# Retention followed by mixture-of-depths: one 128-row matmul for the output in place of two 64-row ones

## The chip, the core and the metric

The kernel runs on one core of a Trainium2 chip. The metric is device time in microseconds (us) for one execution: the median of several runs.

## The reference

Eight batches, eight heads, 576 positions, head dimension 64. The first part is retention in its parallel form: scores `q k^T`, times a decay `gamma_h ** (i - j)` for `i >= j` and 0 elsewhere, times the values. The heads are then put side by side (512 columns), and in every batch the 128 rows with the highest gate score go through a two-layer network of width 1024.

```python
gamma = 1.0 - 2.0 ** (-5.0 - np.arange(H))
rel = pos[:, None] - pos[None, :]
Dmat = np.where(rel >= 0, gamma[:, None, None] ** rel[None, :, :], 0.0)
attn = np.matmul(scale * np.matmul(q, k.T) * Dmat, v)      # per batch and head
x = attn.transpose(0, 2, 1, 3).reshape(B, S, H * D)
...
scores = np.einsum('bsd,d->bs', x, w_gate)
out = x.copy()
for b in range(B):
    top_idx = np.argpartition(-scores[b], capacity)[:capacity]
    xe = x[b, top_idx]
    ye = np.maximum(xe @ w1, 0.0) @ w2
    out[b, top_idx] = xe + sigmoid(scores[b, top_idx])[:, None] * ye
```

## The kernel before

Retention is computed in chunks of 64 positions, nine to a batch (`NC`), 72 in all. A chunk `g` is chunk `c` of batch `b` (`batch(g)`). Within a chunk the kernel takes scores, masks them and multiplies them by the values; what earlier chunks give comes from a 64x64 state per head, the running sum of key times value. The decay is split: values are divided by `gamma ** t` at the chunk's position in its batch (`scaled`, tile `vs`), and the output is multiplied by `gamma ** t` again (`values`).

Two chunks make a step `s` (36 steps, chunks `2s` and `2s + 1`, called `e` = 0 and 1). The 128 partitions hold the positions of a chunk twice over: the lower 64 belong to four of the heads (`HH`) and the upper 64 to the other four (`halves`). A retention matmul is therefore 64 rows by 64 columns and 64 columns of moving data, and runs in one quarter of the TensorE array. Matmuls that stay in their half (`scores`, line 185, and `update`, line 175) use two quarters; those that cross over (`crosswise`, lines 196 and 206, which write the output `y_ps`) use the two others.

`block(s)` writes the order of TensorE's retention work for a step out by hand. It takes two matmul calls at a time from each of two lists. The first, `diagonal`, holds the update of the state with chunk `2s - 1` (8 calls), the scores of step `s` (16) and the update with chunk `2s` (8). The second, `crosswise(s - 1)`, holds masked scores times values for the step before (16 calls) and queries times state (16, fewer where a batch begins). All data is 32-bit float, and each call shows in the trace as two matmul instructions with two weight loads.

The state of all heads accumulates in one PSUM bank, `u_ps`, over a batch. After each update ScalarE copies it to SBUF (`copied`, line 215, tile `st`), and the next update may not write the bank before that copy has read it. The copy of chunk `2s - 1` is issued in the middle of `block(s)`, that of chunk `2s` at its end. VectorE then masks the scores (`masked`, line 242, tile `am`), scales the output (`values`, line 251), and takes the gate scores (line 260). GpSimd scales the values (line 161; in some steps, `by_act`, ScalarE does it with eight instructions, line 157) and issues the stores of the output (line 268). SyncE issues the loads: four transfers of 256 KB for each step (`load`: queries, keys turned, values, keys), eight steps ahead (`AHEAD`, the buffers of the pool `loads`), with a limit on the transfers in flight (`few`).

Between blocks TensorE works off the pieces of the two-layer network of an earlier batch (`up`, line 379, and `down`, line 387, handed out by `some`), and the ranking of a batch's gate scores: `total` (line 293), `spread` (line 308), `compare` (VectorE, line 321), `one_hot` and `rows` (line 342), then an indirect transfer that gathers the chosen rows (`gather`, line 353), `turn` (line 370) and `gates`. `first` and `second` are the hand-ordered steps 4 and 5 at the end of the first batch; `mid`, `early` and `late` are lists of what else is issued in a step. No scheduler reorders anything: each engine runs its instructions in the order in which the program issues them.

Of the kernel before, what the change touches and what calls it, by code (L numbers as in the profile page):

```python
# [35 lines left out]
def kernel(  # L36
# [28 lines left out]
    NK = (NC + 1) // 2  # L65
    W = HH * D
# [2 lines left out]
    col = layout(H, NC, cap)  # L69

    const = ctx.enter_context(tc.tile_pool(name="const", bufs=1))
    loads = ctx.enter_context(tc.tile_pool(name="loads", bufs=8))
    work = ctx.enter_context(tc.tile_pool(name="work", bufs=3))
    psum = ctx.enter_context(tc.tile_pool(name="psum", bufs=2, space=PSUM))

# [52 lines left out]
    slots = const.tile([P, cap], F32, name="slots")  # L128
    eye = const.tile([P, P], F32, name="eye")
    ones = const.tile([P, P], F32, name="ones")  # L130

    def constants():

# [11 lines left out]

    vs, am, sc_ps, y_ps, u_ps, st, xs, sc = {}, {}, {}, {}, {}, {}, {}, {}

    by_act = lambda s: ends[0] <= s < ends[0] + 3 or s - 3 in ends[1:-1]  # L150

    def scaled(s):
        c = batch(2 * s)[1]
        vs[s] = work.tile([P, DM], F32, name="vs")
        if by_act(s):
            for i in range(H):
                nc.scalar.activation(  # L157
                    out=vs[s][:, D * i : D * i + D], in_=raw[s][:, 2, D * i : D * i + D],
                    func=AF.Copy, scale=dec[:, 0, HH * c + i : HH * c + i + 1])
            return  # L160
        nc.gpsimd.tensor_tensor(  # L161
            out=blocks(vs[s]), in0=blocks(raw[s][:, 2, :]),
            in1=dec[:, 0, HH * c : HH * c + H].unsqueeze(2).to_broadcast([P, H, D]), op=OP.mult,
        )

    def update(g):

        (b, c), (s, e) = batch(g), divmod(g, 2)
        if c == NC - 1:
            return  # L170
        if c == 0:
            u_ps[b] = bank("u_ps", "u", 1)
        for h in range(HH):
            for half in halves:
                yield lambda h=h, half=half: nc.tensor.matmul(  # L175
                    u_ps[b][half, where(0, h)], raw[s][half, 3, where(e, h)],
                    vs[s][half, where(e, h)],
                    start=c == 0 and h == 0, stop=c == NC - 2, skip_group_check=True)

    def scores(s):  # L180
        sc_ps[s] = bank("sc_ps", "sc", 2)
        for e in range(2):
            for h in range(HH):
                for half in halves:
                    yield lambda e=e, h=h, half=half: nc.tensor.matmul(  # L185
                        sc_ps[s][half, where(e, h)], raw[s][half, 1, where(e, h)],
                        raw[s][half, 0, where(e, h)],
                        start=True, stop=True, skip_group_check=True)

    def crosswise(s, es=(0, 1)):  # L190
        if es[0] == 0:
            y_ps[s] = bank("y_ps", "y", 2)
        for e in es:
            for h in range(HH):
                for i, half in enumerate(halves):
                    yield lambda e=e, h=h, i=i, half=half: nc.tensor.matmul(  # L196
                        y_ps[s][halves[1 - i], where(e, h)], am[s][half, where(e, h)],
                        vs[s][half, where(e, h)],
                        start=e == 0 and h == 0, stop=False, skip_group_check=True)
        for e in es:  # L200
            g = 2 * s + e
            if batch(g)[1] == 0:
                continue
            for h in range(HH):
                for i, half in enumerate(halves):
                    yield lambda g=g, e=e, h=h, i=i, half=half: nc.tensor.matmul(  # L206
                        y_ps[s][halves[1 - i], where(e, h)], raw[s][half, 0, where(e, h)],
                        st[g - 1][half, where(0, h)], start=False, stop=True,
                        skip_group_check=True)

    def copied(g):
        b, c = batch(g)
        if c < NC - 1:
            st[g] = work.tile([P, W], F32, name="st")
            nc.scalar.copy(out=st[g], in_=u_ps[b][:, :W])  # L215
# [191 lines left out]

    AHEAD = 8  # L410

    def hidden(f):

# [21 lines left out]
    last = B - 1  # L435
    odd = (NC - 2) // 2

    def go(fs):
        for f in fs:
            f()  # L440

    def first():

        s = ends[0] - 1
        block(s)
        masked(s)
        go(crosswise(s, (0,)))
# [8 lines left out]
        go(crosswise(s, (1,)))  # L456
        for k in range(full):
            compare(0, k, 0, P * full)

# [12 lines left out]
    plan(mid, s, rows, 0)  # L472
    plan(mid, s, gather, 0)
    plan(mid, s, store, s - 2, (1,))
    then = {AHEAD: [(upper,)], AHEAD + 1: [(lower, 0)], AHEAD + 2: [(lower, FB // 2)]}
    for x in range(AHEAD, s + AHEAD):
        plan(mid, s, load, x)
        for f, *a in then.get(x, []):
            plan(mid, s, f, *a)
# [35 lines left out]

    bring(table, consts)
    constants()
    for s in range(AHEAD):
        load(s)
    hidden(0)  # L520
    scaled(0)
    for s in range(NS + 1):
        if s > ends[0] + 1 and s + AHEAD - 1 < NS:
            load(s + AHEAD - 1)
        run(before, s)
        if s + 1 < NS and not by_act(s + 1):
            scaled(s + 1)
        if s == ends[0] - 1:
            first()
        elif s == ends[0]:  # L530
            second()
        else:
            block(s)
            if s < NS:
                masked(s)
            run(mid, s)
            if s:
                values(s - 1)
# [4 lines left out]
        if by_act(s + 1) and s + 1 not in vs:  # L543
            scaled(s + 1)
        run(early, s)
        some(share.get(s, 0))
        run(late, s)
# [78 lines left out]
```

## Time and profile before

| | |
|---|---|
| median of 3 runs | 261.44 us (258.08 to 262.19) |
| time of the profiled execution | 259.97 us |
| its span, first to last instruction | 258.2 us |
| TensorE matmuls busy | 225.0 us, 87% (5143 instructions) |
| TensorE weight loads busy | 178.1 us, 69% (5143) |
| VectorE busy | 133.5 us, 52% |
| GpSimd busy | 97.6 us, 38% |
| ScalarE busy | 68.7 us, 27% |
| mean granted TensorE clock | 0.954 |

An engine's busy time is the time in which at least one of its instructions was running. Matmuls overlap: one 64x64 matmul lasts some 0.22 us, but several run at once, so a rate is read from the distance between starts and not from the duration. The clock is given as a share of full speed. In the profile "PE" is TensorE, "PEld" its weight loads, "DVE" VectorE, "ACT" ScalarE, "POOL" GpSimd and "SP" SyncE; "issue" as what ended a wait means that the profile shows no engine or transfer that was waited for.

### The profile page before, as it was taken

Reading aid. Unit: us, or ns where it says so; the run is one execution under the profiler, and the core shown is the slowest. Engines: PE = TensorE matmul, PEld = TensorE weight load, DVE = VectorE, ACT = ScalarE, POOL = GpSimd, SP = SyncE. Lnnn points to the kernel's source line nnn. Section 1 sums busy time; section 2 is a strip of 40 time slices with the busy share of each in tenths; the row PEclk is TensorE's granted clock in tenths of the full one; section 3 lists DMA queues with packets and bytes.
Section 4 is the critical chain, followed back from the end, with each engine's and each line's share of the span. In section 5 each row is a group of like instructions: output and inputs, shape, how many; then the busy total and the mean of one; then the engine's idle time right before and its main releaser. Section 6 shows DMA issues by size and latency. Waiting matters only on the chain.

```text
span 258.2 us, 11519 instructions
## 1 busy us (share of the span) xinstructions
PE 225.0 (87%) x5143; PEld 178.1 (69%) x5143; DVE 133.5 (52%) x354; ACT 68.7 (27%) x230; POOL 97.6 (38%) x132
## 2 busy tenths in 40 slices
PE   0757774896996999889999998999999999999991
PEld 0746654896656797569867976689769966874940
DVE  0344696052993439546835376559465494650201
ACT  2111373131240233313511334133412342221200
POOL 4336304333363541635083722551455505301101
PEclk9995998599797999999999999999999999999997
DMA  6887999999999898799789888986133214201101
GB/s 204 278 256 260 300 371 274 384 326 327 323 287 349 287 313 289 247 310 320 232 282 307 295 280 257 322 287 196 48 83 84 60 27 127 81 3 41 41 0 41
DMA packets 28240, 56.81 MB, mean 220 GB/s; under 512 B 4128, under 2 KB 4256, under 8 KB 28192
## 3 DMA queue, kind: packets, MB, share of 16 engines
q1 hardware_dynamic: 23328, 42.46, 50.3%
q0 software_dynamic: 4864, 13.64, 15.7%
q8 instruction: 40, 0.66, 1.0%
q14 instruction: 8, 0.07, 0.1%
HBM read 44.54 MB, written 11.53 MB: 217 GB/s over the span
## 4 chain that ended last, share of the span: by engine, by line
PE 69%; issue 11%; DMA 9%; ACT 3%; DVE 3%; POOLq 1%; POOL 1%; SPq 0%; ACTq 0%
PE h_ps L379 21%; PE ye_ps L387 16%; PE u_ps L175 10%; PE sc_ps L185 8%; DMA raw<-in_qkvk 7%; PE y_ps L206 5%; PE y_ps L196 3%; PE row_ps L308 3%; DMA xr<-out,idx 2%; PE xg_ps L370 2%; DVE scr L321 2%; ACT vs L157 1%; PE rs_ps L293 1%; PE idx_ps L342 1%; POOLq L564 1%
## 5 line engine op out<-in xcount | busy, mean ns | idle before, releaser
L242 DVE TENSOR_TENSOR am<-sc_ps,table 128x512 f32<-128x512 f32 x36 | 24.9, 691 | 81.4 <-PE sc_ps L185 67.4
L379 PEld LDWEIGHTS h_ps<-xg,w_sb 128*128 128x128 f32 x512 | 61.5, 197 | 5.7 <-issue 3.3
L379 PE MATMUL h_ps<-xg,w_sb 128*128 128x128 f32 x512 | 64.4, 284 | 0.9 <-ACT xg L371 0.7
L387 PE MATMUL ye_ps<-w_sb,hT 128*128 128x512 f32 x128 | 61.4, 611 | 0.0
L185 PE MATMUL sc_ps<-raw 64*64 64x64 f32 x1152 | 45.0, 227 | 10.1 <-DMA raw<-in_qkvk 7.2
L268 POOL DMA_DIRECT2D out<-xs x64 | 39.5, 620 | 35.6 <-DVE xs L251 35.5
L175 PE MATMUL u_ps<-vs,raw 64*64 64x64 f32 x1024 | 45.2, 228 | 6.6 <-ACT st L215 3.1
L185 PEld LDWEIGHTS sc_ps<-raw 64*64 64x64 f32 x1152 | 40.1, 141 | 13.5 <-issue 12.4
L196 PE MATMUL y_ps<-vs,am 64*64 64x64 f32 x1152 | 44.7, 225 | 5.1 <-issue 4.1
L175 PEld LDWEIGHTS u_ps<-vs,raw 64*64 64x64 f32 x1024 | 37.1, 140 | 14.7 <-issue 7.6
L215 ACT COPY st<-u_ps 128x256 f32<-128x256 f32 x64 | 23.8, 372 | 88.0 <-PE u_ps L175 59.7
L196 PEld LDWEIGHTS y_ps<-vs,am 64*64 64x64 f32 x1152 | 38.4, 137 | 5.9 <-issue 4.9
L161 POOL TENSOR_TENSOR vs<-raw,table 128x512 f32<-128x512 f32 x27 | 29.1, 1079 | 34.2 <-DMA raw<-in_qkvk 27.7
L206 PE MATMUL y_ps<-st,raw 64*64 64x64 f32 x1024 | 40.5, 227 | 1.3 <-issue 1.3
L321 DVE SCALAR_TENSOR_TENSOR scr<-row,rs,ahead 128x576 f32<-128x576 f32 (+5 forms) x47 | 34.8, 741 | 8.5 <-ACT row L313 5.8
L206 PEld LDWEIGHTS y_ps<-st,raw 64*64 64x64 f32 x1024 | 36.3, 142 | 0.8 <-issue 0.7
L387 PEld LDWEIGHTS ye_ps<-w_sb,hT 128*128 128x128 f32 x128 | 22.8, 195 | 19.5 <-issue 18.5
L260 DVE SCALAR_TENSOR_TENSOR scr<-xs,table 128x256 f32<-128x256 f32 x72 | 33.7, 468 | 2.5
L353 POOL DMA_INDIRECT xr<-out,idx x8 | 8.4, 1053 | 56.4 <-ACT idx L345 56.4
L381 ACT ACTIVATE hT<-h_ps 128x256 f32<-128x256 f32 x32 | 12.3, 383 | 52.8 <-PE h_ps L379 52.8
L251 DVE TENSOR_TENSOR xs<-y_ps,table 128x512 f32<-128x512 f32 (+1 forms) x37 | 24.7, 668 | 2.8 <-PE y_ps L206 2.5
L393 POOL DMA_INDIRECT out<-o,idx x8 | 9.5, 1189 | 25.6 <-DVE o L392 24.5
(34 smaller groups left out, 110.1 us busy)
## 6 DMA issues: line engine op xcount, KB each, us to landing
raw<-in_qkvk SPq DMA_DIRECT2D x144, 256.0 KB, 4.6
out<-xs POOLq DMA_DIRECT2D x64, 128.0 KB, 4.8
w_sb<-in_w SPq DMA_DIRECT2D x16, 256.0 KB, 5.6
out<-xs POOLq DMA_DIRECT2D x16, 64.0 KB, 4.4
wg<-in_w_gate SPq DMA_DIRECT2D x1, 256.0 KB
table<-in_consts SPq DMA_DIRECT2D x1, 234.5 KB
xr<-out,idx POOLq DMA_INDIRECT x8, 5.8
out<-o,idx POOLq DMA_INDIRECT x8, 4.0
```

The lines of the kernel that those rows point to most:

```text
L161: nc.gpsimd.tensor_tensor(out=blocks(vs[s]), in0=blocks(raw[s][:, 2, :]), in1=dec[:, 0, HH * c : HH * c + H].unsqueeze(2).to_broadcast([P, ...
L175: yield lambda h=h, half=half: nc.tensor.matmul(u_ps[b][half, where(0, h)], raw[s][half, 3, where(e, h)], vs[s][half, where(e, h)], start= ...
L185: yield lambda e=e, h=h, half=half: nc.tensor.matmul(sc_ps[s][half, where(e, h)], raw[s][half, 1, where(e, h)], raw[s][half, 0, where(e, h ...
L196: yield lambda e=e, h=h, i=i, half=half: nc.tensor.matmul(y_ps[s][halves[1 - i], where(e, h)], am[s][half, where(e, h)], vs[s][half, where ...
L206: yield lambda g=g, e=e, h=h, i=i, half=half: nc.tensor.matmul(y_ps[s][halves[1 - i], where(e, h)], raw[s][half, 0, where(e, h)], st[g - 1 ...
L242: nc.vector.tensor_tensor(out=blocks(am[s]), in0=blocks(sc_ps[s]), in1=causal.unsqueeze(1).to_broadcast([P, H, C]), op=OP.mult)
L251: nc.vector.tensor_tensor(out=blocks(xs[s])[:, i0:i1, :], in0=blocks(y_ps[s])[:, i0:i1, :], in1=dec[:, 1, HH * c + i0 : HH * c + i1].unsqu ...
L260: nc.vector.scalar_tensor_tensor(scr, xs[s][:, W * e : W * e + W], 1.0, wgh, op0=OP.mult, op1=OP.mult, accum_out=sc[b][:, c : c + 1])
L268: nc.gpsimd.dma_start(out=outs[b][C * c : C * c + 2 * C, W * i : W * i + W] .rearrange("(c p) d -> p c d", c=2), in_=xs[s][half, :].rearra ...
L321: nc.vector.scalar_tensor_tensor(scr[:n, : j1 - j0], row[b][:n, j0:j1], rs[b][:n, k : k + 1], ahead[:n, at + j0 : at + j1], op0=OP.subtrac ...
L379: nc.tensor.matmul(t[:, a, :], w1_sb[:, d, P * (f + a) : P * (f + a) + P], xg[b][:, d, :], start=d == 0, stop=d == KD - 1)
L387: nc.tensor.matmul(ye[b], hT[b][:, a, :], w2_sb[:, a, :], start=a == 0, stop=a == FB - 1)
```

## The change

Masked scores and queries are put one under the other in the 128 partitions, and so are values and state, so that one matmul with 128 rows gives what two with 64 rows gave before. For this a step's tile `raw` has six slots in place of four. For the lower half the slots 2 and 3 are loaded with queries and values, for the upper half the slots 4 and 5. The masked scores of one half are written by VectorE beside the queries of the other (`masked`, slots `QA`), and the copy of the state goes beside the values of the other half (`copied`, slots `VS`), which takes two ScalarE instructions of 64 partitions in place of one of 128. The weight `1 / gamma ** t` is no longer put on the values: for the scores it is in a table `decay` (mask times weight, made by VectorE in five instructions, `decays`), and for the state it is put on the keys, in place, by the engine that scaled the values before. The mask becomes two VectorE instructions. Scores now cross over between halves, so that scores and updates use the four quarters together, and the output's matmuls come after both. The loads are six steps ahead, with eight issued at the start; a load is still four transfers of 256 KB, now in the order keys turned, queries with values (one transfer for each half), keys.

```diff
-    loads = ctx.enter_context(tc.tile_pool(name="loads", bufs=8))
+    loads = ctx.enter_context(tc.tile_pool(name="loads", bufs=6))
...
+    KT, KN = 0, 1
+    QA, VS = {1: 2, 0: 4}, {0: 3, 1: 5}
...
     def load(s):
-        x = loads.tile([P, 4, DM], F32, name="raw")
-        for a in range(4):
-            bring(x[:, a, :], qkvk[s, :, a * DM : (a + 1) * DM], few=6 if ends[0] < s <= FEW else 4)
+        x = loads.tile([P, 6, DM], F32, name="raw")
+        few = 6 if ends[0] < s <= FEW else 4
+        src = qkvk[s].rearrange("p (a d) -> p a d", d=DM)
+        bring(x[:, KT, :], src[:, 1, :], few)
+        for p, half in enumerate(halves):
+            bring(x[half, QA[1 - p] : VS[p] + 1, :], src[half, 0:3:2, :], few)
+        bring(x[:, KN, :], src[:, 3, :], few)
...
+    def decays(c0, c1):
+        n = HH * (c1 - c0)
+        nc.vector.tensor_tensor(
+            out=decay[:, c0:c1, :].rearrange("p c (h d) -> p (c h) d", d=C),
+            in0=causal.unsqueeze(1).to_broadcast([P, n, C]),
+            in1=dec[:, 0, HH * c0 : HH * c1].unsqueeze(2).to_broadcast([P, n, C]), op=OP.mult)
...
     def scaled(s):
...
+        keys = raw[s][:, KN, :]
...
         nc.gpsimd.tensor_tensor(
-            out=blocks(vs[s]), in0=blocks(raw[s][:, 2, :]),
+            out=blocks(keys), in0=blocks(keys),
...
     def update(g):
...
-                    u_ps[b][half, where(0, h)], raw[s][half, 3, where(e, h)],
-                    vs[s][half, where(e, h)],
+                    u_ps[b][half, where(0, h)], raw[s][half, KN, where(e, h)],
+                    raw[s][half, VS[p], where(e, h)],
...
+    def copied(g):
+        (b, c), (s, e) = batch(g), divmod(g + 1, 2)
+        if c < NC - 1:
+            for p, half in enumerate(halves):
+                nc.scalar.copy(out=raw[s][halves[1 - p], VS[p], W * e : W * e + W],
+                               in_=u_ps[b][half, :W])
...
     def scores(s):
...
-                        sc_ps[s][half, where(e, h)], raw[s][half, 1, where(e, h)],
-                        raw[s][half, 0, where(e, h)],
+                        sc_ps[s][half, where(e, h)], raw[s][halves[1 - p], KT, where(e, h)],
+                        raw[s][halves[1 - p], QA[p], where(e, h)],
...
     def crosswise(s, es=(0, 1)):
         for e in es:
+            some = batch(2 * s + e)[1] > 0
             for h in range(HH):
-                for i, half in enumerate(halves):
-                    yield lambda e=e, h=h, i=i, half=half: nc.tensor.matmul(
-                        y_ps[s][halves[1 - i], where(e, h)], am[s][half, where(e, h)],
-                        vs[s][half, where(e, h)],
-                        start=e == 0 and h == 0, stop=False, skip_group_check=True)
-        for e in es:
-            g = 2 * s + e
-            if batch(g)[1] == 0:
-                continue
-            for h in range(HH):
-                for i, half in enumerate(halves):
-                    yield lambda g=g, e=e, h=h, i=i, half=half: nc.tensor.matmul(
-                        y_ps[s][halves[1 - i], where(e, h)], raw[s][half, 0, where(e, h)],
-                        st[g - 1][half, where(0, h)], start=False, stop=True,
-                        skip_group_check=True)
+                for p, half in enumerate(halves):
+                    at = slice(0, P) if some else half
+                    nc.tensor.matmul(
+                        y_ps[s][halves[1 - p], where(e, h)], raw[s][at, QA[p], where(e, h)],
+                        raw[s][at, VS[p], where(e, h)],
+                        start=e == 0 and h == 0, stop=True, skip_group_check=True)
...
     def block(s, cross=True):
-        def diagonal():
+        def states():
             if s:
                 yield from update(2 * s - 1)
             if s < NS:
-                yield from scores(s)
                 yield from update(2 * s)
-        a = diagonal()
-        b = crosswise(s - 1) if s and cross else iter(())
+        a = states()
+        b = scores(s) if s < NS else iter(())
         n = 0
         while True:
             some = [f for f in (next(a, None), next(a, None), next(b, None), next(b, None)) if f]
...
             n += 1
             if n == HH and s:
                 copied(2 * s - 1)
         if s < NS:
             copied(2 * s)
+        if s and cross:
+            crosswise(s - 1)

     def masked(s):
-        am[s] = work.tile([P, DM], F32, name="am")
-        nc.vector.tensor_tensor(
-            out=blocks(am[s]), in0=blocks(sc_ps[s]),
-            in1=causal.unsqueeze(1).to_broadcast([P, H, C]), op=OP.mult)
+        c = batch(2 * s)[1]
+        for p, half in enumerate(halves):
+            nc.vector.tensor_tensor(
+                out=raw[s][half, QA[p], :], in0=sc_ps[s][half, :],
+                in1=decay[half, c : c + 2, :].rearrange("p c d -> p (c d)"), op=OP.mult)
...
-    AHEAD = 8
+    AHEAD, FIRST = 6, 8
...
-    for s in range(AHEAD):
+    decays(0, 2)
+    for s in range(FIRST):
         load(s)
...
+        if s < 4:
+            decays(2 * s + 2, 2 * s + 4)
```

More of the change, by code (lines that the diff above doesn't have):

```diff
@@ L130 @@
     ones = const.tile([P, P], F32, name="ones")
+    decay = const.tile([P, NC + 1, W], F32, name="decay")
     def constants():
@@ L144, in constants @@
         nc.scalar.activation(out=warm, in_=ones[:, :1], func=AF.Sigmoid)
-    vs, am, sc_ps, y_ps, u_ps, st, xs, sc = {}, {}, {}, {}, {}, {}, {}, {}
+    sc_ps, y_ps, u_ps, xs, sc = {}, {}, {}, {}, {}
+    def decays(c0, c1):
[4 more added lines that the diff above has]
+            in1=dec[:, 0, HH * c0 : HH * c1].unsqueeze(2).to_broadcast([P, n, C]), op=OP.mult)
     by_act = lambda s: ends[0] <= s < ends[0] + 3 or s - 3 in ends[1:-1]
+    done = set()
     def scaled(s):
         c = batch(2 * s)[1]
-        vs[s] = work.tile([P, DM], F32, name="vs")
+        done.add(s)
+        keys = raw[s][:, KN, :]
         if by_act(s):
             for i in range(H):
-                nc.scalar.activation(
-                    out=vs[s][:, D * i : D * i + D], in_=raw[s][:, 2, D * i : D * i + D],
-                    func=AF.Copy, scale=dec[:, 0, HH * c + i : HH * c + i + 1])
+                at = slice(D * i, D * i + D)
+                nc.scalar.activation(out=keys[:, at], in_=keys[:, at], func=AF.Copy,
+                                     scale=dec[:, 0, HH * c + i : HH * c + i + 1])
             return
         nc.gpsimd.tensor_tensor(
-            out=blocks(vs[s]), in0=blocks(raw[s][:, 2, :]),
+            out=blocks(keys), in0=blocks(keys),
             in1=dec[:, 0, HH * c : HH * c + H].unsqueeze(2).to_broadcast([P, H, D]), op=OP.mult,
@@ L173, in update @@
         for h in range(HH):
-            for half in halves:
-                yield lambda h=h, half=half: nc.tensor.matmul(
-                    u_ps[b][half, where(0, h)], raw[s][half, 3, where(e, h)],
-                    vs[s][half, where(e, h)],
+            for p, half in enumerate(halves):
+                yield lambda h=h, p=p, half=half: nc.tensor.matmul(
+                    u_ps[b][half, where(0, h)], raw[s][half, KN, where(e, h)],
+                    raw[s][half, VS[p], where(e, h)],
                     start=c == 0 and h == 0, stop=c == NC - 2, skip_group_check=True)
+    def copied(g):
[4 more added lines that the diff above has]
+                               in_=u_ps[b][half, :W])
     def scores(s):
@@ L183, in scores @@
             for h in range(HH):
-                for half in halves:
-                    yield lambda e=e, h=h, half=half: nc.tensor.matmul(
-                        sc_ps[s][half, where(e, h)], raw[s][half, 1, where(e, h)],
-                        raw[s][half, 0, where(e, h)],
+                for p, half in enumerate(halves):
+                    yield lambda e=e, h=h, p=p, half=half: nc.tensor.matmul(
+                        sc_ps[s][half, where(e, h)], raw[s][halves[1 - p], KT, where(e, h)],
+                        raw[s][halves[1 - p], QA[p], where(e, h)],
                         start=True, stop=True, skip_group_check=True)
@@ L193, in crosswise @@
         for e in es:
+            some = batch(2 * s + e)[1] > 0
             for h in range(HH):
-                for i, half in enumerate(halves):
-                    yield lambda e=e, h=h, i=i, half=half: nc.tensor.matmul(
-                        y_ps[s][halves[1 - i], where(e, h)], am[s][half, where(e, h)],
-                        vs[s][half, where(e, h)],
-                        start=e == 0 and h == 0, stop=False, skip_group_check=True)
-        for e in es:
-            g = 2 * s + e
-            if batch(g)[1] == 0:
-                continue
-            for h in range(HH):
-                for i, half in enumerate(halves):
-                    yield lambda g=g, e=e, h=h, i=i, half=half: nc.tensor.matmul(
-                        y_ps[s][halves[1 - i], where(e, h)], raw[s][half, 0, where(e, h)],
-                        st[g - 1][half, where(0, h)], start=False, stop=True,
-                        skip_group_check=True)
[L211 to L215, printed above, removed]
+                for p, half in enumerate(halves):
+                    at = slice(0, P) if some else half
[3 more added lines that the diff above has]
+                        start=e == 0 and h == 0, stop=True, skip_group_check=True)
     def block(s, cross=True):
-        def diagonal():
+        def states():
             if s:
@@ L238, in block @@
             copied(2 * s)
+        if s and cross:
+            crosswise(s - 1)
     def masked(s):
-        am[s] = work.tile([P, DM], F32, name="am")
-        nc.vector.tensor_tensor(
-            out=blocks(am[s]), in0=blocks(sc_ps[s]),
-            in1=causal.unsqueeze(1).to_broadcast([P, H, C]), op=OP.mult)
+        c = batch(2 * s)[1]
+        for p, half in enumerate(halves):
+            nc.vector.tensor_tensor(
+                out=raw[s][half, QA[p], :], in0=sc_ps[s][half, :],
+                in1=decay[half, c : c + 2, :].rearrange("p c d -> p (c d)"), op=OP.mult)
     def values(s, es=(0, 1)):
@@ L436 @@
     odd = (NC - 2) // 2
-    def go(fs):
-        for f in fs:
-            f()
     def first():
@@ L446, in first @@
         masked(s)
-        go(crosswise(s, (0,)))
+        crosswise(s, (0,))
         values(s - 1)
@@ L455, in first @@
         spread(0, columns(full, NK))
-        go(crosswise(s, (1,)))
+        crosswise(s, (1,))
         for k in range(full):
@@ L474 @@
     plan(mid, s, store, s - 2, (1,))
-    then = {AHEAD: [(upper,)], AHEAD + 1: [(lower, 0)], AHEAD + 2: [(lower, FB // 2)]}
-    for x in range(AHEAD, s + AHEAD):
+    then = {FIRST: [(upper,)], FIRST + 1: [(lower, 0)], FIRST + 2: [(lower, FB // 2)]}
+    for x in range(FIRST, s + AHEAD):
         plan(mid, s, load, x)
@@ L540 @@
                     store(s - 1)
+        if s < 4:
+            decays(2 * s + 2, 2 * s + 4)
         if s == 2:
             nc.vector.tensor_copy(out=place, in_=place_f)
-        if by_act(s + 1) and s + 1 not in vs:
+        if by_act(s + 1) and s + 1 not in done:
             scaled(s + 1)
@@ L586, in turned @@
     def turned(x):
-        return (x.reshape(B, 2, HH, NC, C, D)[:, ::-1].transpose(0, 3, 1, 5, 2, 4)
+        return (x.reshape(B, 2, HH, NC, C, D).transpose(0, 3, 1, 5, 2, 4)
                 .reshape(NS, 2, 2, D, HH, C).transpose(0, 2, 3, 1, 4, 5))
```

## The prediction

> **What bounds the kernel now.** I read the page first (busy shares, slices, clock), then the stretches, then the order of time in one step, then the waits.
>
> ```profile
> span 258.2 us, 11519 instructions
> PE 225.0 (87%) x5143; PEld 178.1 (69%) x5143; DVE 133.5 (52%) x354; ACT 68.7 (27%) x230; POOL 97.6 (38%) x132
> PE   0757774896996999889999998999999999999991
> PEclk9995998599797999999999999999999999999997
> ...
> q8 instruction: 40, 0.66, 1.0%
> ```
>
> TensorE is full in nearly every slice after the seventh (46 us on); before that the loads come in. One stretch says it in numbers:
>
> ```profile
> 85.00:236.00 151.00, 146.75 (x3324) 115.43 (x3322) 88.71 (x234) 43.41 (x148) 61.43 (x81) 1.00 0.63 203
> ```
>
> Columns: window, length, then busy us of PE, PEld, DVE, ACT, POOL, clock, DMA share, GB/s. TensorE is busy 97% at full clock, VectorE 59%, ScalarE 29%, DMA 63%. So what an edit does to TensorE's own order of work goes to the span one for one; the others have room.
>
> One retention block, from the order of time:
>
> ```profile
> 142.16 0.27 PE L175 MATMUL u_ps<-vs,raw 64*64 64x64 f32 x2
> 142.17 0.27 PE L196 MATMUL y_ps<-vs,am 64*64 64x64 f32 x2
> 142.26 0.22 PE L175 MATMUL u_ps<-vs,raw 64*64 64x64 f32 x2
> ...
> 142.61 0.22 PE L175 MATMUL u_ps<-vs,raw 64*64 64x64 f32 x2
> 142.67 0.23 PE L185 MATMUL sc_ps<-raw 64*64 64x64 f32 x2
> ...
> 142.94 0.37 ACT L215 COPY st<-u_ps 128x256 f32<-128x256 f32 x1 [0.20 <-PE u_ps L175]
> ...
> 143.60 0.63 PE L175 MATMUL u_ps<-vs,raw 64*64 64x64 f32 x16
> 144.17 2.05 PE L379 MATMUL h_ps<-xg,w_sb 128*128 128x128 f32 x16
> ```
>
> Four matmul instructions (two of each list, four quarters of the array) start every 0.058 us (142.61 to 142.67); the sixteen updates alone go two at a time: (0.63 - 0.22) / 7 = 0.058 a pair. So the price is 0.058 per round, whether two or four run in it. And see the state's copy at 142.94: it lies under the scores, and the second update starts at 143.60, long after the copy ended at 143.31.
>
> **The change, part by part.** The base is the profiled execution: 259.97 us, span 258.2.
>
> *Matmuls.* A full block had 128 instructions in fours, 32 rounds, 1.86 us. Now updates and scores make 64 in fours (16 rounds), and the output 32 instructions of 128 rows by 64 columns in twos (16 rounds): 1.86 us again. A quarter of the instructions goes, but no array time: gain 0. No row has a 128-row, 64-column matmul with 64 moving columns. Bounds over the 31 blocks after the load-bound start: the rate of four per round (0.46 less per block, -14.3) and each one alone (0.93 more, +28.8). I take 0, by the nearest rows: the 16 updates in pairs, and
>
> ```profile
> 147.94 0.28 PE L293 MATMUL rs_ps<-sc,table 128*64 128x5 f32 x4
> 148.15 0.27 PE L175 MATMUL u_ps<-vs,raw 64*64 64x64 f32 x2
> ```
>
> four instructions of 128 rows by 64 columns, each 0.20 long, start within 0.08 us; with weights loaded one after another it would be 3 x 0.058 = 0.17.
>
> The Trainium skill speaks against this. "TensorE: Matmul & The Clock Gate", Part 3, says that a weight load overlaps a running matmul only where the row groups differ, and 128-row matmuls share them all; by that rule the pairs would fall apart and the sum would be 28.8 higher. The trace differs: sixteen h_ps matmuls of 128 rows start (2.05 - 0.38) / 15 = 0.11 us apart, each with its own weight load of all rows, while one load lasts 0.197. I go by the row.
>
> *The wait for the state.* This is the large term. Before, 16 scores lay between the two updates of a block. Now `states` gives update 2s - 1 and at once update 2s, in the same PSUM bank, and the copies between them are two instructions. TensorE takes its work in order, so scores and output behind the second update wait with it. From the start of the last round of the first update: 0.22 (that matmul) + 0.11 (142.83 to 142.94, until ScalarE starts) + 0.37 (first copy) + 0.27 (second: 0.37 less 0.10, since copies of 0.59 and 0.22 us take 0.71 together) + 0.06 until TensorE starts, as in
>
> ```profile
> 8.84 0.37 ACT L215 COPY st<-u_ps 128x256 f32<-128x256 f32 x1 [5.48 <-PE u_ps L175]
> 9.27 0.33 PE L175 MATMUL u_ps<-vs,raw 64*64 64x64 f32 x2 [0.47 <-ACT st L215]
> ```
>
> = 1.03, less the round of 0.058 that would have passed, plus 0.05 for the slow first round after a stop (142.16 to 142.26 against 0.058): 1.02 us. It falls in steps where chunks 2s - 1 and 2s are in one batch and neither is its last: 28, three of them in the load-bound start: 25 x 1.02 = +25.5. Bounds: one copy's time in all (0.75, +18.7); copies without overlap, once in two behind a relu of 0.38 (1.3, +32.5). A gain is excluded. The wait at the block's end (copies of chunk 2s) is covered by the output's 0.93 us and mostly by network pieces of 1.7 us or more.
>
> *Changes of shape.* From 64x64 to 128-row shapes the step is 0.16 (last update 144.01, h_ps 144.17) against 0.058, and the first round after is 0.10. Each block has one more such change: 0.15 x 31, and one more in four blocks where a batch begins at e = 1: +5.2. Bounds 0 and 10.
>
> *Instruction supply.* TensorE's only waits in 46 to 236 us worth a term are these:
>
> ```profile
> PE sc_ps L185 <- issue: 2.9, 3, 1.2
> PE y_ps L196 <- issue: 2.7, 2, 2.2
> PE u_ps L175 <- issue: 2.2, 1, 2.2
> PE y_ps L206 <- issue: 0.2, 1, 0.2
> ```
>
> 8.0 us, all inside retention blocks, waiting for nothing that the profile shows. The instruction queue moved 0.66 MB in 40 packets, 64 bytes for each of TensorE's 10286 matmuls and loads: 16 KB, 256 instructions, a packet, just what a block used up in 1.9 us. I read the gaps as TensorE waiting for its next packet. A block now uses 192 in some 3 us, so I expect most of it to go: -6. The two gaps of 2.2 us were followed by half clock:
>
> ```profile
> 63.00:68.00 5.00, 5.00 (x108) 3.68 (x105) 3.18 (x9) 1.45 (x4) 0.75 (x2) 0.66 0.98 313
> 80.00:85.00 5.00, 5.00 (x116) 4.13 (x117) 2.25 (x6) 0.96 (x2) 1.59 (x3) 0.66 0.86 296
> ```
>
> 5 x 0.34 = 1.7 us lost each; I take one back. Together -7.7, bounds -11.4 and 0.
>
> *The start.* GpSimd now scales the keys, the last of four transfers, where it scaled the third: about +1.0 on the chain to the first ranking. The mask of step 4 is two instructions (0.69 more), and the copies of chunk 11 stand between ScalarE's eight scalings and the ranking's matmuls: +0.5. Together +2.2, bounds 0 and 4.
>
> *At nothing.* VectorE's second mask instruction is 0.69 x 36 = 25 us, hidden in its 41% idle time; the output needs it a step later (6 us), now even later in the block; without that cover it would be 0.7 a step. I keep +0.5 for one place, the last batch's ranking at 216.5, where only two network pieces stand before it. The five `decays` (0.7 each) fall in the load-bound start. Loads: still four SP issues a step, 1 MB, the same 2 KB pieces; each waits for a buffer freed five steps before use instead of seven, some 30 us against a landing of 4.6; uncovered it is 4 us a step, as at the start. SP's network weights stand behind loads 6 and 7, which now wait for steps 1 and 2 (done by 16 us, and issued after 24). POOL's order is as it was, its scaling as long as before.
>
> Sum: 259.97 + 0 + 25.5 + 5.2 - 7.7 + 2.2 + 0.5 = 285.7, say 286. The median shown is 1.5 above this execution; I leave that in the range.
>
> **Rivals.**
> - *The pairs run one by one.* For: all rows are shared. Against: the h_ps and rs_ps rows. 285.7 + 28.8 = 314.5.
> - *The new gaps halve the clock.* For: after 2.2 us gaps it was half for 3.4 us (the dips in PEclk). Against: a gap of 1.2 (the longest for sc_ps, at 110 us) left it at 1.00. 25 x 1.7 more: 328. The Trainium skill ("TensorE: Matmul & The Clock Gate", "Why this matters for your kernels") asks only that no gap between bursts exceeds about 3 us; by that rule no term is due here or for the old gaps, and mine for one dip would be 0; by the rows 2.2 is already too much.
> - *Not slower: the updates don't stop TensorE.* Its place is the second update of a block; if what it waits for is over when it comes, the term of 25.5 falls and 260.2 is left. It decides below 0.2 us a block. For: the waits for the copy that the whole trace shows are 3.1 us, though each block's end hands one to the next block's start. Against: there pieces of the network lie between, and at 9.27 TensorE stood idle for just this copy.
> - *Faster:* that, and all of the instruction supply's 11.4 us with no price for shapes: 251.
>
> **How the numbers follow.** Forecast 0.70, pairs one by one 0.10, clock 0.07, wait absent 0.09, faster 0.04. No change can be told from this measurement within about 2% (5 us). The terms' bounds around 286: the wait -7 and +7, shapes -5 and +5, supply -4 and +8, start -2 and +2; not all at one end, so 271 to 302 for the likeliest alone. To leave no more than 2 in 10 out I reach up to the pairs one by one: 269 to 316. Faster 0.04, same 0.08 (the wait absent, mostly), slower 0.88.
>
> **What would show it.** Right: a group of waits of u_ps for ScalarE's copies, 25 or more at 0.6 to 0.9 us each, in all over 18; copies 128 in number, back to back; y_ps pairs 0.058 apart; "issue" gaps under 3 us; VectorE near 160 us busy, still not the bound. Wrong: no such group, or y_ps starting singly, 0.058 or more apart (then the array, not the wait, is the price), or half-clock stretches after 85 us. If TensorE waits for VectorE's masks or for loads, my covers were wrong.

## The result, and the profile after

The changed kernel takes 300.34 us (median of 6 runs, 298.72 to 302.18) against 261.81 us (6 runs): slower, the ratio being 1.156 with a 95% interval of 1.148 to 1.165. The forecast was 286, with a range of 269 to 316. Executions of a kernel fall into a faster and a slower state: medians here are of all runs, ratios of the faster ones alone.

From the page of the changed kernel:

```profile
span 298.8 us, 9740 instructions
PE 239.0 (80%) x4119; PEld 186.9 (63%) x4119; DVE 163.3 (55%) x395; ACT 93.1 (31%) x294; POOL 96.9 (32%) x132
PE   0685665888689888789879887888888887999992
PEclk9999657599899999799979999799999999799999
...
q8 instruction: 32, 0.52, 0.7%
```

A fifth of TensorE's instructions is gone, and yet its slices fell from 9 to 8 nearly throughout, and new 7s stand in the clock row. The same stretch as before (columns as there):

```profile
85.00:236.00 151.00, 129.80 (x2389) 101.34 (x2388) 88.78 (x214) 50.43 (x159) 58.65 (x77) 0.97 0.71 211
```

TensorE fell from 97% to 86% busy; VectorE is at 59% as before, ScalarE at 33%. No other engine became the bound, so TensorE waits. The waits view for TensorE from 60 us on (us in total, times, longest) says for which instruction:

```profile
PE u_ps L198 <- ACT raw L208: 11.0, 6, 2.1
PE u_ps L198 <- issue: 9.3, 9, 1.3
PE u_ps L198 <- POOL raw L184: 8.6, 7, 2.1
```

22 waits, 28.9 us, all of `update`, under three names. The order of time shows what most of these names hide. An ordinary block, from the last round of its first update on:

```profile
200.22 0.23 PE L198 MATMUL u_ps<-raw 64*64 64x64 f32 x2
200.61 0.74 ACT L208 COPY raw<-u_ps 64x256 f32<-64x256 f32 x2 [0.27 <-DMA raw<-in_qkvk]
201.45 0.27 PE L198 MATMUL u_ps<-raw 64*64 64x64 f32 x2 [1.00 <-POOL raw L184]
```

The view names GpSimd, whose scaling ended at 201.21; but the two copies ended at 201.35, TensorE started 0.10 later, and in 21 of the 22 blocks the start stands 0.05 or 0.10 us behind the copies. The one other is at 80.44 us: its copies ended at 79.06, GpSimd's scaling of the keys at 80.38, so there the name is right. A named releaser is an inference: look at what ended just before the start each time.

Five times (119, 149, 186, 216 and 251 us) the gap is twice as long. One of them:

```profile
119.06 0.23 PE L198 MATMUL u_ps<-raw 64*64 64x64 f32 x2
119.15 1.02 POOL L373 DMA_INDIRECT xr<-out,idx  x1 [7.71 <-ACT idx L365]
120.58 0.74 ACT L208 COPY raw<-u_ps 64x256 f32<-64x256 f32 x2 [1.71 <-PE u_ps L198]
121.38 0.37 PE L198 MATMUL u_ps<-raw 64*64 64x64 f32 x2 [2.08 <-ACT raw L208]
```

The update ended at 119.29 and ScalarE was free, but the copies started 1.29 us later: the trace has TensorE's post (the semaphore update that tells ScalarE that the bank may be read) at 120.56. Between the two, GpSimd was preparing the gather (119.15 to 120.17). And the matmul at 121.38 is 0.37 long instead of 0.27: the clock is at half.

### The profile page after: what moved, and what is told of

The parts are those of the page before. It is cut to its first block, busy times and chain, and to the rows that moved or that the text cites. A ratio compares the mean times of both kernels' runs of the same rounds, so it can differ in the third digit from the quotient of the medians.

```text
span 298.8 us, 9740 instructions
## 1 busy us (share of the span) xinstructions
PE 239.0 (80%) x4119; PEld 186.9 (63%) x4119; DVE 163.3 (55%) x395; ACT 93.1 (31%) x294; POOL 96.9 (32%) x132
## 4 chain that ended last, share of the span: by engine, by line
DMA 35%; PE 31%; issue 17%; DVE 6%; POOL 5%; ACT 3%; POOLq 1%; SPq 1%; ACTq 0%; DVEq 0%
DMA raw<-in_qkvk 26%; PE h_ps L399 12%; PE y_ps L230 5%; PE u_ps L198 5%; DMA out<-xs 5%; PE ye_ps L407 5%; DMA xr<-out,idx 3%; DVE raw L262 3%; DVE xs L271 2%; POOL raw L184 2%; POOL out L288 2%; PE row_ps L328 2%; ACT raw L181 1%; ACT raw L208 1%; PE sc_ps L216 1%
## 5 line engine op out<-in xcount | busy, mean ns | idle before, releaser
L262 DVE TENSOR_TENSOR raw<-sc_ps,decay 64x512 f32<-64x512 f32 x72 | 49.6, 689 | 90.2 <-issue 48.7
L198 PE MATMUL u_ps<-raw 64*64 64x64 f32 x1024 | 49.3, 241 | 46.7 <-POOL raw L184 19.7
L198 PEld LDWEIGHTS u_ps<-raw 64*64 64x64 f32 x1024 | 40.1, 149 | 59.0 <-POOL raw L184 21.8
L208 ACT COPY raw<-u_ps 64x256 f32<-64x256 f32 x128 | 47.0, 367 | 86.0 <-PE sc_ps L216 26.8
L216 PE MATMUL sc_ps<-raw 64*64 64x64 f32 x1152 | 52.8, 240 | 0.6 <-DMA raw<-in_qkvk 0.6
L230 PE MATMUL y_ps<-raw 128*64 128x64 f32 (+1 forms) x1152 | 49.8, 246 | 2.6 <-DVE raw L262 2.6
L230 PEld LDWEIGHTS y_ps<-raw 128*64 128x64 f32 (+1 forms) x1152 | 43.8, 157 | 5.8 <-issue 2.8
L184 POOL TENSOR_TENSOR raw<-raw,table 128x512 f32<-128x512 f32 x27 | 28.4, 1051 | 38.5 <-DMA raw<-in_qkvk 15.4
L401 ACT ACTIVATE hT<-h_ps 128x256 f32<-128x256 f32 x32 | 12.3, 384 | 56.9 <-PE h_ps L399 56.9
L181 ACT ACTIVATE raw<-raw,table 128x64 f32<-128x64 f32 x72 | 18.2, 336 | 1.6 <-DMA raw<-in_qkvk 1.5
L412 DVE SCALAR_TENSOR_TENSOR o<-ye_ps,gate,xr 128x512 f32<-128x512 f32 x8 | 6.0, 750 | 22.7 <-issue 12.7
```

The source lines that it names most:

```text
L184: nc.gpsimd.tensor_tensor(out=blocks(keys), in0=blocks(keys), in1=dec[:, 0, HH * c : HH * c + H].unsqueeze(2).to_broadcast([P, H, D]), op= ...
L198: yield lambda h=h, p=p, half=half: nc.tensor.matmul(u_ps[b][half, where(0, h)], raw[s][half, KN, where(e, h)], raw[s][half, VS[p], where( ...
L208: nc.scalar.copy(out=raw[s][halves[1 - p], VS[p], W * e : W * e + W], in_=u_ps[b][half, :W])
L216: yield lambda e=e, h=h, p=p, half=half: nc.tensor.matmul(sc_ps[s][half, where(e, h)], raw[s][halves[1 - p], KT, where(e, h)], raw[s][halv ...
L230: nc.tensor.matmul(y_ps[s][halves[1 - p], where(e, h)], raw[s][at, QA[p], where(e, h)], raw[s][at, VS[p], where(e, h)], start=e == 0 and h ...
L262: nc.vector.tensor_tensor(out=raw[s][half, QA[p], :], in0=sc_ps[s][half, :], in1=decay[half, c : c + 2, :].rearrange("p c d -> p (c d)"), ...
```

## The experiments

My theory was that the second update's wait for the state's copies costs nearly everything. The rivals were the 128-row matmuls with their changes of shape, and the loads that are only six steps ahead. Ratios are to the kernel before, run on the same chip beside the variant, with their 95% intervals. Line numbers are those of the kernel named.

**1. The wait taken away.** The copies in mid-block read a table:

```diff
-                               in_=u_ps[b][half, :W])
+                               in_=u_ps[b][half, :W] if g % 2 == 0 else decay[half, 0, :])
```

> The copies in the middle of a block read a constant table and not the state (so the state that the output sees in every second chunk is not the right one); as many instructions on every engine, but the second update waits for nothing. Theory (the wait for the state's copies is the cost): of the 300.3 us go 22 gaps at 1.0 us idle plus 0.16 of lost overlap, six longer ones at about 2.2, and some 5 us of half clock: 258 to 266 us, and the gaps of u_ps are gone. Rival (128-row matmuls and the changes of shape): at least 290. Rival (loads only six steps ahead): at least 290.

Measured 263.94 us, 1.020 (1.005 to 1.035). After 85 us no u_ps wait of 0.2 us or more is left. So 36.4 of the 38.5 us go with the wait and what follows from it, and 128-row matmuls, shapes, loads and lighter instruction supply together leave some 2%. Both rivals fall as the main cost. From 60 us on, the two largest waits of TensorE are now:

```profile
PE u_ps L198 <- POOL raw L184: 5.1, 3, 2.3
PE sc_ps L216 <- DMA raw<-in_qkvk: 2.3, 1, 2.3
```

All four lie between 60 and 80 us: TensorE waits for loads and for keys not yet scaled. Before the change no wait in this stretch had these names. I read this as loads that come late, which in the changed kernel the wait for the copies mostly covers.

**2. The wait put into the kernel before.** Only the order of its list changes:

```diff
-                yield from scores(s)
                 yield from update(2 * s)
+                yield from scores(s)
```

> The kernel before, with one change: both updates come first in the list and the scores after them. Nothing is stacked. Theory: the second update waits for one copy of 0.37 us: 0.22 + 0.11 + 0.37 + 0.1 less one round, about 0.75 us in 25 blocks, some 19 us: 277 to 286 us, more if gaps meet the gather. Rivals (128-row matmuls, six steps of loads ahead): no change, 262.

Measured 278.55 us, 1.078 (1.053 to 1.104). A block of it:

```profile
99.96 0.37 ACT L215 COPY st<-u_ps 128x256 f32<-128x256 f32 x1 [0.30 <-PE u_ps L175]
100.43 0.27 PE L175 MATMUL u_ps<-vs,raw 64*64 64x64 f32 x2 [0.56 <-POOL vs L161]
```

One copy, a gap of 0.56, and 17 us with nothing stacked. The order of the updates alone costs that.

**3. The length of the copies.** In the changed kernel, one copy of 128 partitions holds the bank; the slots beside the values are filled from a table behind it:

```diff
+            if g % 2:
+                nc.scalar.copy(out=work.tile([P, W], F32, name="st"), in_=u_ps[b][:, :W])
...
-                               in_=u_ps[b][half, :W])
+                               in_=decay[half, 0, :] if g % 2 else u_ps[b][half, :W])
```

> The changed kernel with the state's copy in the middle of a block as one instruction of 128 partitions into a tile that nobody reads; the two slots beside the values are filled from a constant table behind it (every second state is not the right one). The second update waits for one copy of 0.37 us instead of two of 0.75 together. Theory: 22 gaps of 0.62 instead of 1.00, 8 us less: 288 to 294 us. If the late post beside the gather has to do with the two copies of 64 partitions, the five gaps of 2.0 go to 0.6 as in the second experiment, and the half clock after them: 280 to 286. Rival (the gap isn't the length of the copies): 300.

Measured 288.84 us, 1.104 (1.094 to 1.114).

```profile
115.57 0.37 ACT L208 COPY st<-u_ps 128x256 f32<-128x256 f32 x1 [2.01 <-PE u_ps L198]
...
116.04 0.27 PE L198 MATMUL u_ps<-raw 64*64 64x64 f32 x2 [0.56 <-issue]
...
121.85 0.37 ACT L208 COPY st<-u_ps 128x256 f32<-128x256 f32 x1 [1.74 <-PE u_ps L198]
...
122.27 0.27 PE L198 MATMUL u_ps<-raw 64*64 64x64 f32 x2 [1.73 <-ACT st L208]
```

The ordinary gap is the 0.56 of experiment 2, so the second copy of 64 partitions is 0.44 us of an ordinary block's gap of 1.00. The long gaps only fell from 2.0 to 1.7: the late post is still there and hasn't to do with the two copies.

I also tried to run the two halves at once, the second on VectorE:

```diff
-                nc.scalar.copy(out=raw[s][halves[1 - p], VS[p], W * e : W * e + W],
-                               in_=u_ps[b][half, :W])
+                (nc.vector.tensor_copy if p and g % 2 else nc.scalar.copy)(
+                    out=raw[s][halves[1 - p], VS[p], W * e : W * e + W], in_=u_ps[b][half, :W])
```

> The changed kernel with the second half of each copy in the middle of a block done by VectorE beside ScalarE, so that the two halves run at once. Theory: the wait is the length of the copies, so each of 22 gaps loses up to 0.37 us (8 us in all), less where VectorE is busy with comparisons of the ranking and takes the copy late: 290 to 297 us, gaps of 0.63 instead of 1.00 where VectorE is free. If the gap were set by something else than the copies: no change of the gaps, 300.

Measured 312.19 us, 1.194 (1.185 to 1.203): a miss.

```profile
181.97 0.36 ACT L208 COPY raw<-u_ps 64x256 f32<-64x256 f32 x1 [0.36 <-POOL raw L184]
182.36 0.43 DVE L208 COPY raw<-u_ps 64x256 f32<-64x256 f32 x1 [3.25 <-ACT raw L208]
182.89 0.27 PE L198 MATMUL u_ps<-raw 64*64 64x64 f32 x2 [1.08 <-issue]
```

By the trace VectorE waited for ScalarE's copy, so the halves still ran one after the other, 0.43 us in place of 0.37. Where VectorE was in a comparison the gap grew to 1.6 or 1.7, once (at 88 us) to 3.1; the six gaps of 2.1 to 2.3 are the late post again. It tells nothing of halves run at once.

**4. The gather moved.** Five long gaps lie beside a gather:

```diff
-        plan(late, s + 2, gather, b)
+        plan(mid, s + 3, gather, b)
```

> The changed kernel with the gather of batches 1 to 6 issued one block later on GpSimd. In the changed kernel's trace five of the six longest gaps (2.0 to 2.1 us) are blocks in which TensorE's post for the copies came 1.2 us late while GpSimd prepared the gather, and half-clock stretches follow them. If the gather is what makes them long: five gaps fall to 1.0 and four stretches of half clock after 85 us go: 287 to 294 us. Rival (ScalarE's eight scalings in the same steps): no change, 300.

Measured 295.29 us, 1.137 (1.114 to 1.161): some 1 us above the range of the theory, and the interval overlaps that of the changed kernel, so the total doesn't settle it. The trace shows:

```profile
119.42 0.74 ACT L208 COPY raw<-u_ps 64x256 f32<-64x256 f32 x2 [0.46 <-PE u_ps L198]
120.22 0.27 PE L198 MATMUL u_ps<-raw 64*64 64x64 f32 x2 [0.83 <-ACT raw L208]
...
121.47 1.05 POOL L373 DMA_INDIRECT xr<-out,idx  x1 [0.17 <-issue]
```

In the same five steps the gap is 0.83, with ScalarE's scalings where they were, so these alone are not the cause. The four stretches of half clock after 85 us (3.4 us each, from 121, 152, 189 and 254 us) are gone; one new one stands at 193 us, behind a wait of 2.5 us for the gathered rows. Part of the gain is given back in such waits:

```profile
PE xg_ps L390 <- DMA xr<-out,idx: 6.8, 4, 2.6
```

Why the post is late is not settled. In experiment 2 the update ends at the same moment (0.14 us after the gather's start, at 82, 112 and 139 us), and the copy starts 0.2 us after the update's end. What differs there, beside the stacking, wasn't isolated.

**5. The pairs.** All heads of one half first, then the other:

```diff
-            for h in range(HH):
-                for p, half in enumerate(halves):
+            for p, half in enumerate(halves):
+                for h in range(HH):
```

> The changed kernel with the output's matmuls of one half of the heads first and those of the other half after them, so that neighbours go to the same columns of the array and cannot run side by side. If the pairs run side by side in the changed kernel (0.93 us for 32 instructions): 16 rounds more in each of 31 blocks, 28.8 us more, 329 us, and an output stretch of 1.8 us. If a weight load that shares all rows with a running matmul already kept them apart: no change, 300.

Measured 310.45 us, 1.175 (1.162 to 1.188). The output of a block, first in the changed kernel, then here:

```profile
115.43 1.15 PE L230 MATMUL y_ps<-raw 128*64 128x64 f32 x32
```

```profile
115.55 1.54 PE L230 MATMUL y_ps<-raw 128*64 128x64 f32 x32
```

From first to last start that is 0.93 (15 steps, the first of 0.11, the others of 0.058) and 1.32. In the changed kernel the two of a pair start 0.006 apart; here the first four and the last four matmuls start singly, a step apart, so neighbours in the same columns go one by one, and in the changed kernel the pairs do run side by side, with all rows shared. I expected 329 us and a stretch of 1.8 us, and both were too much: in the middle of the stretch nine pairs still start together. I read them as the second half of the first chunk beside the first half of the second.

**6. Fewer instructions in the kernel before.** Its queries-times-state matmuls are left out; the other list keeps the block at 32 rounds:

```diff
-                        start=e == 0 and h == 0, stop=False, skip_group_check=True)
+                        start=e == 0 and h == 0, stop=True, skip_group_check=True)
...
-            if batch(g)[1] == 0:
+            if g >= 0:
                 continue
```

> The kernel before without the matmuls of queries with the state (line 206; the output lacks what earlier chunks give). A block still has 32 rounds of 0.058 us, since the list of updates and scores sets them, but 192 instructions for 256. Theory (the issue gaps in blocks, 8.0 us in the kernel before, are TensorE waiting for its next packet of instructions): the gaps after 85 us (3.4 us) go and those before shrink: 252 to 258 us. Rival (the gaps come from transfers of data): no change, 260 to 262.

Measured 253.32 us, 0.969 (0.961 to 0.976). From 46 us on, TensorE's "issue" waits are:

```profile
PE sc_ps L185 <- issue: 1.5, 4, 0.4
...
PE y_ps L196 <- issue: 0.4, 1, 0.4
```

1.9 us in place of 8.0. The gaps follow the number of instructions, as a supply of 256 a packet would have it. The times of the instruction queue's packets in the traces say so too. In the kernel before, each of the seven waits that make up the 8.0 us ends 1.2 to 1.5 us after a packet has landed (one landed at 110.34 us, and the wait ended at 111.69), while packets come 5 to 6 us apart on average. The five waits of 0.4 us that are left here don't stand at this distance.

**7. Start and loads.** On top of experiment 1, loads eight ahead (`bufs=8`, `AHEAD, FIRST = 8, 8`) and, apart from that, the keys as the first transfer and the turned keys as the last.

> The kernel of the first experiment (copies in mid-block read a constant table, so every second state is wrong) with loads eight steps ahead as before the change. The first experiment was 263.9 us with gaps of 1.1 to 2.3 us at 60 to 78 us in which TensorE waited for loads and scaled keys, and a half clock after them. If six steps ahead cause these: they go, 254 to 259 us. Rival (the transfers are just as late with eight, since the weights of the network stand between them): 262 to 265.

> The kernel of the first experiment (every second state wrong as there) with the keys as the first of a load's four transfers and the turned keys as the last. If the later scaling of the keys costs the start (first h_ps at 50.7 us against 46.1 before the change): 1 to 4 us less, 260 to 263. Rival (the start is longer for other reasons): no change, 264.

Measured 269.17 us (1.030, 1.024 to 1.036) and 272.95 us (1.042, 1.034 to 1.050): both slower than experiment 1, and both misses. The first h_ps matmul stays at 51.0 and 51.3 us (50.7 in experiment 1, 46.1 before the change). Neither six steps nor the order of transfers explains the later start, and why these two are slower than experiment 1 is open. One candidate for the start wasn't tested, VectorE's added work (`decays` and the second mask). From 19 to 33 us VectorE is busy for 12.3 us in experiment 1 and 8.0 us before the change, and its first comparison of the ranking starts at 34.1 us against 30.9: 3.2 of the 4.6 us are there by then.

**8. A cover for the wait.** The output's matmuls go between the two updates:

```diff
...
+        b = list(scores(s)) if s < NS else []
+        if s:
+            together(update(2 * s - 1), iter(b[:H]))
+            copied(2 * s - 1)
+            b = b[H:]
+            if cross:
+                crosswise(s - 1)
         if s < NS:
+            together(update(2 * s), iter(b))
             copied(2 * s)
-        if s and cross:
-            crosswise(s - 1)
```

(`together` takes two calls at a time from each of its two lists, as the loop of `block` did.)

> The changed kernel with the output's matmuls between the two updates of a block (first update with half of the scores, output, second update with the other half). The copies then lie under 16 rounds of output (0.93 us) and a change of shape. Theory: the gaps of u_ps shrink below 0.2 us; one more change of shape (0.15 x 31 = 4.6): 260 to 270 us. Rival (128-row matmuls and shapes): 300 or more, since one change more comes in. Rival (loads six ahead): 300.

Measured 274.11 us, 1.057 (1.039 to 1.075), above the 260 to 270 of the theory. The waits for the copies are gone after 60 us but for 0.4 us. In their place:

```profile
PE idx_ps L358 <- DVE hot L350: 3.2, 4, 0.9
PE rs_ps L309 <- DVE scr L276: 2.7, 2, 1.4
```

Scores now end with the block, VectorE's masks come later, and what stands behind them in its order comes later too. I then issued the one-hot ahead of the masks, and the store ahead of the gather (the text calls the experiment above the third):

```diff
-        plan(mid, s + 2, one_hot, b)
+        plan(before, s + 2, one_hot, b)
...
+        plan(late, s + 2, store, s + 1)
         plan(late, s + 2, gather, b)
-        plan(late, s + 2, store, s + 1)
```

> The third experiment (output between the two updates) with the one-hot of a batch issued on VectorE before the masks of its step, and the store before the gather on GpSimd. There TensorE still waited 3.2 us for the one-hot and 2.7 for gate scores, since masks and outputs now come later and VectorE takes its work in order. Theory: the 3.2 us and some half clock go: 268 to 272 us. It isn't expected to beat the kernel before, as blocks have the same 32 rounds and two more changes of shape (0.3 x 31 = 9 us). Rival (something else holds it at 274): no change.

Measured 284.38 us, 1.087 (1.078 to 1.095): a miss. The wait for the one-hot went, but TensorE now waited 9.0 us for gathered rows (xg_ps, from 46 us on); that the gather behind the store makes them late is my reading, not tested by itself. No version here that keeps the whole computation beats the kernel before.

## Why the prediction was right, point by point

*Array time.* Right: 16 rounds for updates with scores, 16 for the output, 0.93 us each. The "pairs run one by one" rival is out by experiment 5. The rule of the Trainium skill that I weighed ("TensorE: Matmul & The Clock Gate", Part 3: a weight load overlaps a running matmul only where row groups differ; for a load into the background weight buffer the same Part allows it too) would, taken alone, have kept the pairs apart; here the trace shows 128-row pairs at 0.058 us a pair, and the measurement decides.

*The wait.* The mechanism was right, the term too small: 25.5 was predicted, with bounds of 18.7 and 32.5, and 36.4 went in experiment 1. The total stayed in its range all the same, and that is partly luck: the range reached up to 316 for the pairs running one by one, which they don't. Three sizes were off. First, from the start of the first update's last round to the second update an ordinary block took 1.23 us (200.22 to 201.45) and not 1.03: ScalarE started 0.39 after that round (I had 0.33), the copies from PSUM didn't overlap (0.74 together, I had 0.64), and TensorE started 0.10 after them, not 0.06. Second, the late post beside the gather, some 1.05 us in five of the blocks and in one at the start, was in none of my lists. Third, the half clock behind these gaps. The rivals "not slower" and "faster" are out: the second update stopped TensorE 22 times after 60 us.

*The clock rival* was partly right, and one of my signs for "wrong" did come: half-clock stretches after 85 us, four of them. In the changed kernel four of the five stretches of half clock after 60 us follow such gaps of 2.0 us, the fifth one of 2.13 at 78 us; none follows the ordinary gaps of 0.83 to 1.28. That agrees with what the gaps of 2.2 did before the change, and with the rows I preferred to the 3 us of the Trainium skill ("TensorE: Matmul & The Clock Gate", "Why this matters for your kernels").

*Shapes.* Right as far as the trace shows single starts: from the last round of scores to the first of the output some 0.15 us in place of 0.058, and 0.11 for that first round.

*Supply.* The gaps went: of the 3.6 us of "issue" waits from 85 to 236 us, experiment 1 has none. The -7.7 is of the size that experiment 6 gives for a like cut in the kernel before, -8.6.

*The start* was mis-sized. With two of the waits I had 2.2 + 2.0 us there; the first h_ps came 8.3 us later (54.35 against 46.07), 4.6 of it without the wait. I had put the five `decays` at nothing there; whether they are part of the 4.6 wasn't tested (experiment 7).

*At nothing.* VectorE reached 163 us (I had near 160) and TensorE hardly waited for it (2.6 us for masks before 60 us, nothing of 0.3 or more after). This cover held after the start. Loads: after 60 us 0.6 us of waits under their own name, and 1.4 us behind the copies at 80 us for keys not yet scaled. But much of this cover was the wait itself: with the wait gone, experiment 1 has 7.4 us of such waits. My sign for "right", 25 or more waits for the copies of 0.6 to 0.9, was off in form: 22 after 60 us, longer, and two thirds under other engines' names.

## What to carry to other kernels

Fewer matmuls are no gain where the array's rounds set the pace: count rounds, not instructions. Ask of each reordering what used to lie between a producer and the reuse of its PSUM bank; here 16 scores hid a copy, and moving them cost more than a quarter of the matmul instructions gave. A new gap has a second price once it meets another (a gather's preparation, the clock gate), so the sum of single gaps can fall short: here five long gaps were each followed by 3.4 us at half clock, by my estimate 1.7 us more apiece.

## What the runs showed of the hardware

- A ScalarE copy of 64 partitions by 256 from PSUM takes as long as one of 128 (0.37 us), and two in a row take 0.74 (changed kernel and experiment 3).
- In the changed kernel gaps of 2.0 us on TensorE were mostly followed by 3.4 us at half clock, in one case not (216 us); gaps up to 1.3 us never were after 85 us. The limit isn't sharp: in experiment 3 three of six gaps of 1.7 us were followed by half clock, in experiment 4 a gap of 2.6 us was not (129 us), and in experiment 2 a gap of 1.3 us at 68 us, with one of 0.5 soon after it, was.
- The stretches of half clock of the changed kernel after 60 us begin at 80.07, 121.03, 151.75, 189.30 and 254.15 us, whole multiples of 3.41 us from one another.
- TensorE's "issue" waits in the kernel before ended 1.2 to 1.5 us after a packet of the instruction queue had landed (seven of seven from 46 to 236 us).
- TensorE's post after an update came over 1 us late in six blocks of the changed kernel, with the gather being prepared on GpSimd, and nearly on time in the second experiment in the same position.
- The two column halves of the array take 128-row matmuls side by side, 32-bit, with weights loaded under them: the two of a pair start 0.006 us apart, pairs 0.058.
